# Gradient turns moved from TensorE to DMA transposes, and weight loads cut into pieces, in the training step of a four-layer stack

## The chip, the cores and the metric

The kernel runs on one core of one Trainium2 chip. The metric is the device time of one execution in microseconds (us). The core has a TensorE (PE, with its weight loads shown as PEld), a VectorE (DVE), a ScalarE (ACT), a GpSimd (POOL), a SyncE (SP), and 16 DMA engines.

## The reference

```python
def A(x, wqkv, wo):                       # linear attention, H=32 heads of 16
    q, k, v = split(x @ wqkv)
    phi = lambda t: where(t > 0, t + 1, exp(t)) + 1e-6
    kv, z = phi(k)^T v, sum(phi(k))       # per head
    return concat(phi(q) kv / (phi(q) z + 1e-6)) @ wo
def B(x, w_gate, w_up, w_down):           # gated feed-forward
    return (sigmoid(x @ w_gate) * (x @ w_up)) @ w_down
def fwd(x):
    x = x + A(layernorm(x)); x = x + B(layernorm(x))
    x = x + A(layernorm(x)); x = x + B(layernorm(x))
    return x
out, vjp = jax.vjp(fwd, x, wqkv, wo, w_gate, w_up, w_down)
return out, *vjp(grad_out)
```

This is a sketch of the reference in short form. x is 1 x 2048 x 512 in bfloat16, the feed-forward width is 1376. Both attention layers (numbered 0 and 2) share weights, and so do both feed-forward layers (1 and 3). The outputs are the stack's output and the gradients of x and of the five weight matrices.

## The kernel before

Tokens lie in 16 tiles of P = 128 (NST = 16), four to a batch of BT = 512 (NB = 4, NBLK = 4 batches); 512 features are NDC = 4 blocks of 128; the width 1376 is NFC = 11 chunks of 128. PE, ACT, DVE and POOL work in an order that is written out by hand. All DMAs are issued on SP's one queue; their order there comes from the scheduler by its own estimates, a DMA waits until the one eight before it on SP has landed (eight lanes), and SP issues in order, so that a DMA that waits holds up all behind it. In the trace landings come in order of issue. tile_pool buffers ("bufs") bound how far a producer may run ahead.

The stages in order, with the profile's times in us: forward of layers 0 and 1 until 215, of layers 2 and 3 until 407; backward of layer 3 (BBwd, `first`) 407 to 532; backward of layer 2 (ABwd, "A2") first half 530 to 612, second half to 694; then weight-gradient work, backward of layer 1 (BBwd) 735 to 855; backward of layer 0 (ABwd, "A0") first half 855 to 943, second half to 1000; the remaining weight gradients to the end.

*Forward.* `ab_fwd` does a feed-forward layer in pairs of token tiles; `gu` (L1070) makes g and u for a unit of two chunks (CUNITS, six units to a pair), ACT makes ssd_t and oms from g (L1086, L1087), DVE and POOL hhT and the second half of ssd_t (L1088, L1089), and ssd_t goes to sv_ssd in DRAM (L1092). ssd_t has 3 buffers, tr_stg (L1097, the staging of transposed operands that are stored as sv_hdd and sv_hdl) has 2. In layer 3 `turn_weights` issues, one at a time, the jobs of `wT_dmas_b` (L455), which load transposed weights for the backward pass: among them wuT and wgT, in pieces of chunks 0 to 5 (768 KB) and 6 to 9 (512 KB).

*Feed-forward backward.* `BBwd.run` goes over four batches and 11 chunks u each. `D(n)` makes dhh_ps (L1385) from the turned gradient gT and the weights, two chunks ahead (LOOK = 2), so that the next batch's gT is first read at u = 9; `H` accumulates dh_ps (L1417). gT is made by `make_gT` (L1347): eight PE transposes for each half batch and an ACT copy, at u = 5 and 6 (7 and 8 for the last batch of layer 3). Its source gstage is loaded from grad_out in layer 3 (`load_g`), and in layer 1 cast by ACT from the fp32 residual gradient (`cast_g`, u = 1 to 4), which also stores it to sv_gbf in DRAM (L1345). While H runs, sv_hdd and sv_hdl are stored from tr_stg (L1042), and ssd and h_ld are loaded.

*Attention backward, first half.* `ABwd.first` goes over 16 token tiles (steps): `dp_make` (L1758, dp_ps from gT and MT), `gT_make` for the next tile (four PE transposes L1750, an ACT copy L1751, two buffers), `g_cast` two tiles ahead (ACT, the bfloat16 gradient), and the elementwise work on phq_ld, which is stored as sv_dq (L1823). pqn is loaded by batches (L1837). Each step ends with a *unit* of weight-gradient work from `p2_gen`: 16 matmuls p_ps<-p_set (L1694), four units to a job; p_set holds a job's operand and is loaded two jobs ahead into two buffers (from sv_dkT as four transposing DMAs L1560, from sv_hdd L1571, from sv_hdl as four DMAs L1578); the results go out by dw_stg and dwp (L1648). At the end comes GT_ps (L1870), a sum over all 16 g tiles. The second half loads turned operands by transposing DMAs (pkT_ld L1900, dqT_ld L1904).

Of the kernel before, what the change touches and what calls it, by code (L numbers as in the profile page):

```python
# [9 lines left out]
BF16 = mybir.dt.bfloat16  # L10
# [444 lines left out]
def wT_dmas_b(k):  # L455
    nc = k.nc
    view = lambda d: d.rearrange("(c p) f -> p c f", p=P)
    parts, h = [], F // 2
    for r0, r1, c0 in ((0, h, 0), (h, F, WDT)):
        parts.append((k.wdT[:, WDT:NDC, r0:r1], k.w_in["wd"][r0:r1, WDT * P:D],  # L460
                      [(view(k.wT["wdT"][c0 * P:(c0 + 2) * P, :]), k.wdT[:, c0:c0 + 2, :])]))
    jobs = wT_dmas(k, parts)
    for nm, t in (("wu", k.wuT), ("wg", k.wgT)):
        for c, e in ((0, 6), (6, NFC - 1)):
            jobs.append(lambda nm=nm, t=t, c=c, e=e: nc.sync.dma_start(out=t[:, c:e, :],
                                                                       in_=view(k.wT[nm + "T"][c * P:e * P, :])))
        jobs.append(lambda nm=nm, t=t: nc.sync.dma_start(out=view(k.wT[nm + "T"][(NFC - 1) * P:, :]),
                                                         in_=t[:, NFC - 1:, :]))
    return jobs
# [580 lines left out]
def ab_fwd(k, A, ln, fill, nxt=None, out_cb=None, bwd=None):  # L1050
# [3 lines left out]
    with ExitStack() as ctx:  # L1054
        work = ctx.enter_context(tc.tile_pool(name=f"bf_work{l}", bufs=2, reuse_waits="tile"))
        wide = ctx.enter_context(tc.tile_pool(name=f"bf_wide{l}", bufs=2, reuse_waits="tile"))
        hhT = {}

        def gu(st, nt, c0, nch, between=None):
# [16 lines left out]
            if held:  # L1076
                ssd = bwd.ssd[0][:, c0:c0 + nch, :, off:off + n]
            else:
                ssd_f = work.tile([P, 2 * BT], BF16, name="ssd_t", bufs=3)
                ssd = ssd_f[:, 0:2 * w].rearrange("p (c a t) -> p c a t", c=nch, a=2)  # L1080
# [14 lines left out]
        def trans(B, g):  # L1095
            c0, nch = CG[g]
            block_transposes(k, work, sv, 0, B, g, hhT[B][:, c0:c0 + nch, :], bufs=2)  # L1097

# [56 lines left out]
        for i in range(1, NPAIR):  # L1155
# [7 lines left out]
            nt = 1 if i < NPAIR - 2 else 2  # L1163
            gu(st, 2, *CUNITS[0])
            A.attn_y(st + 2, "t")
            A.pair_front1(i + 2)
# [7 lines left out]
            if l == 3 or i % 2 == 0:  # L1174
                turn_weights()
                if l == 3 and i > 3:
                    turn_weights()
            if i > 1:
                down_mm(st - 2)
            ln.apply(st + 2)  # L1180
            if last:
                trans(NBLK - 1, 0)
            gu(st, 2, *CUNITS[3])
            down_mm(st - 1, "t")
            ln.apply(st + 3)
# [3 lines left out]
            if last:  # L1189
                trans(NBLK - 1, 1)  # L1190
                if bwd is not None:
                    bwd.make_gT(0, 0)
            gu(st, 2, *CUNITS[4])
            ln.stage_T([st + 2, st + 3], bank="t")
            A.pair_front3(i + 2)
            after(st - 2)
            if last and bwd is not None:
                bwd.make_gT(0, 1)
            gu(st, 2, *CUNITS[5])
            fills((nf + 1) // 3, "vector")  # L1200
            if l == 1 and last:
# [108 lines left out]
class BBwd:  # L1310
# [20 lines left out]
    def load_g(self, B):  # L1331
# [3 lines left out]
        t = self.G[B] = self.G.get(B) or self.alloc(False, "stg", [P, NB, D], "gstage", 2)  # L1335
        if self.first:
            nc.sync.dma_start(out=t[:], in_=dram_batch(k.g_in, B))

    def cast_g(self, B, j):
# [91 lines left out]
    def run(self, nxt, hooks={}, rest=None, fill=None):  # L1431
# [3 lines left out]
        with ExitStack() as ctx:  # L1435
# [27 lines left out]
            for B in range(NBLK):  # L1463
                end = B == NBLK - 1
                for u in range(NFC):
                    n = B * NFC + u
                    close = u == NFC - 1
                    behind = self.first and B == 2 and u == 9
                    if close and end:
                        nxt.gT_make(0, "ln")  # L1470
                    if not close and not behind:
                        self.D(n + self.LOOK)
                    self.H(B, u)
                    if behind:
                        self.D(n + self.LOOK)
                    if close and not end:
# [10 lines left out]
                    if not end:  # L1487
# [3 lines left out]
                        if late and u == 3:  # L1491
                            self.load_g(3)
                        if u in ((7, 8) if late else (5, 6)):
                            self.make_gT(B + 1, 0 if u in (5, 7) else 1)
                    if u in (7, 8):
# [227 lines left out]
class ABwd:  # L1723
# [20 lines left out]
    def gT_make(self, st, bank="t"):  # L1744
        k = self.k
        if st < NST:
            self.gTs[st] = self.hold.tile([P, NDC, P], BF16, name="gT", bufs=2)
            ps = ps_tile(k, bank, [P, NDC, P], BF16, "gT_ps")
            for c in range(NDC):
                k.nc.tensor.transpose(ps[:, c, :], self.g[st][:, c * P:(c + 1) * P], k.ident[:])  # L1750
            k.nc.scalar.copy(self.gTs[st][:], ps[:])  # L1751

    def dp_make(self, st):
# [19 lines left out]
    def first(self, fill):  # L1773
# [10 lines left out]
        with tc.tile_pool(name=f"ab_all{l}", bufs=1, reuse_waits="tile") as allp, \  # L1784
# [41 lines left out]

            self.g_cast(2)
            load_ph(0)
            load_ph(1)
            weights = self.weights = k.load_a_weights(l)  # L1830
            for st in range(NST):
# [9 lines left out]
                if st > 0:  # L1841
                    self.dp_make(st)
                    self.gT_make(st + 1)
                    self.g_cast(st + 2)
                    self.cneg_make(st, small.tile([P, H], F32, name="cneg"))
                T["cneg"] = self.cneg
                T["cneg_bf"] = small.tile([P, H], BF16, name="cneg_bf", bufs=DZLAG + 3)
# [189 lines left out]

DZLAG = 4
SMALL = (("G", D), ("kvbd", P), ("dkvbd", P))

# [65 lines left out]
```

## Time and profile before

| | us |
|---|---|
| runs | 1132.63, 1131.10, 1133.29 |
| median of the runs | 1132.63 |
| profiled execution | 1131.85 |
| span of the profiled execution | 1130.1 |
| busy PE, PEld, DVE, ACT, POOL | 1094.4, 673.3, 718.7, 501.9, 468.1 |
| granted clock of TensorE, mean | 0.997 |

The span runs from the first to the last instruction in the trace of one execution; 1.75 us of its time lie outside. A group's row has the line, engine, operation and tiles, then its busy time, the mean ns of one, and the idle time in front of it with what ended it. A row of a timeline has start, duration, engine, line, tiles and how many instructions it holds; in brackets is the idle time before the first, with its releaser. In SP's rows the duration is the time that issuing took; a row of DMA issues ends with the median time from issue to landing. The clock of TensorE is granted by a throttle, as a share of full speed.

### The profile page before, as it was taken

To read this page: it belongs to the slowest core of one execution; us is meant where nothing else is said; L and a number is where in the kernel's file an instruction comes from. 1 tells how busy PE (TensorE), PEld (TensorE's weight loads), DVE (VectorE), ACT (ScalarE), POOL (GpSimd) and SP (SyncE) were. 2 spreads that over 40 slices of the span, in tenths; PEclk is the share of its full clock that TensorE was granted. 3 is DMA by queue.
4 is the path that set the end of the run, shared out by engine and by line. 5 is a ranking of instruction groups with operands and counts; after the bars stand their busy time and mean duration, and the time that the engine had idled before them with its cause. 6 is when DMAs were issued, how large, how long until landed. Compare 5 with 4: busy or idle time off the path is not lost. (4 is left out here: it accounts for less than half of the span.)

```text
span 1130.1 us, 20199 instructions
## 1 busy us (share of the span) xinstructions
PE 1094.4 (97%) x7453; PEld 673.3 (60%) x7556; DVE 718.7 (64%) x1263; ACT 501.9 (44%) x924; POOL 468.1 (41%) x627
## 2 busy tenths in 40 slices
PE   7999999999999899999999999999999999999998
PEld 4467767546776654444665556544446756555577
DVE  7887887888678567776993640057778955642221
ACT  4676656557656533444552441145545523420001
POOL 3738776433766445776110440047772101420000
PEclk9999999999999999999999999999999999999999
DMA  7955657695666768978789967887768999958997
GB/s 218 319 169 160 199 177 222 198 263 177 173 217 187 235 201 265 303 232 278 214 235 265 280 192 253 296 283 225 224 214 223 268 276 253 258 194 272 274 253 166
DMA packets 342612, 263.02 MB, mean 233 GB/s; under 512 B 105648, under 2 KB 321136, under 8 KB 342512
## 3 DMA queue, kind: packets, MB, share of 16 engines
q1 hardware_dynamic: 342512, 261.72, 79.0%
q8 instruction: 59, 0.97, 0.4%
q14 instruction: 41, 0.34, 0.1%
HBM read 122.62 MB, written 119.47 MB: 214 GB/s over the span
## 5 line engine op out<-in xcount | busy, mean ns | idle before, releaser
L1694 PE MATMUL p_ps<-p_set,p_a 128*128 128x384 bf16 (+2 forms) x1792 | 264.6, 304 | 3.3 <-DMA p_set<-sv_hdd 1.5
L1694 PEld LDWEIGHTS <-p_a 128*128 128x128 bf16 x1792 | 168.7, 96 | 87.2 <-issue 3.4
L1393 POOL TENSOR_TENSOR dd<-dhb,ssd 128x512 bf16<-128x512 bf16 x84 | 96.7, 1156 | 106.1 <-ACT dhb L1391 103.9
L1392 DVE TENSOR_TENSOR dd<-dhh_ps,ssd 128x512 bf16<-128x512 f32 x85 | 57.2, 679 | 123.1 <-ACT dhb L1391 121.3
L1417 PE MATMUL dh_ps<-wuT,dd 128*128 128x512 bf16 (+1 forms) x340 | 129.0, 379 | 0.7
L1089 POOL TENSOR_TENSOR ssd_t<-hhT,oms 128x512 bf16<-128x512 bf16 (+1 forms) x92 | 99.7, 1092 | 71.8 <-DVE hhT L1088 50.4
L1417 PE MATMUL dh_ps<-wgT,dd 128*128 128x512 bf16 (+1 forms) x325 | 123.3, 380 | 0.0
L1417 PEld LDWEIGHTS <-dd 128*128 128x128 bf16 x680 | 66.3, 98 | 79.7
L1070 PE MATMUL g_ps<-hT,wg 128*128 128x256 bf16 (+1 forms) x792 | 93.6, 262 | 6.5 <-ACT oms L1087 5.4
L1709 DVE TENSOR_TENSOR dw_stg<-p_ps,dw_stg 128x384 bf16<-128x384 f32 (+2 forms) x76 | 32.0, 438 | 106.4 <-PE p_ps L1694 99.1
L1070 PE MATMUL u_ps<-hT,wu 128*128 128x256 bf16 (+1 forms) x792 | 93.5, 262 | 3.0 <-DVE hhT L1088 3.0
L1391 ACT CAST dhb<-dhh_ps 128x512 bf16<-128x512 f32 x84 | 48.7, 588 | 99.5 <-PE dhh_ps L1385 86.6
L1088 DVE TENSOR_TENSOR hhT<-u_ps,ssd_t 128x512 bf16<-128x512 f32 (+1 forms) x92 | 57.5, 629 | 51.5 <-ACT ssd_t L1086 49.2
L1086 ACT ACTIVATE ssd_t<-g_ps 128x512 bf16<-128x512 f32 (+1 forms) x92 | 51.7, 562 | 86.6 <-PE g_ps L1070 44.4
L1039 DVE STREAM_TRANSPOSE tr_stg<-dd 128x768 f32<-128x768 f32 (+1 forms) x62 | 86.6, 1437 | 1.1
L1070 PEld LDWEIGHTS <-wg 128*128 128x128 bf16 x792 | 70.1, 98 | 27.2 <-issue 8.0
L1385 PE MATMUL dhh_ps<-gT,wdT 128*128 128x512 bf16 x301 | 77.2, 379 | 1.6 <-DVE dd L1392 0.7
L1105 PE MATMUL y_ps<-wd,hhT 128*128 128x512 bf16 (+1 forms) x337 | 77.7, 380 | 0.8
L1070 PEld LDWEIGHTS <-wu 128*128 128x128 bf16 x792 | 70.9, 98 | 12.0 <-issue 4.6
L1711 ACT CAST dw_stg<-p_ps 128x384 bf16<-128x384 f32 (+2 forms) x76 | 28.0, 385 | 88.6 <-PE p_ps L1694 83.8
L1385 PEld LDWEIGHTS <-wdT 128*128 128x128 bf16 x352 | 33.8, 97 | 41.7 <-issue 3.8
L516 POOL TENSOR_TENSOR rstd_all<-rstd_all,neghalf 128x1 f32<-128x1 f32 x64 | 37.9, 592 | 47.7 <-DVE rstd_all L515 43.1
(256 smaller groups left out, 1919.3 us busy)
## 6 DMA issues: line engine op xcount, KB each, us to landing
sv_hdd<-tr_stg SPq DMA_DIRECT2D x72, 384.0 KB, 4.6
p_set<-sv_hdd SPq DMA_DIRECT2D x18, 1536.0 KB, 7.4
sv_ssd<-ssd_t SPq DMA_DIRECT2D x74, 256.0 KB, 2.6
ssd<-sv_ssd SPq DMA_DIRECT2D x23, 768.0 KB, 5.2
h_ld<-sv_h SPq DMA_DIRECT2D x30, 256.0 KB, 4.1
sv_hdl<-tr_stg SPq DMA_DIRECT2D x24, 256.0 KB, 4.8
p_a<-sv_h SPq DMA_DIRECT2D x12, 512.0 KB, 6.5
p_set<-sv_hdl SPq DMA_DIRECT2D x24, 256.0 KB, 4.9
```

The source lines that it names most:

```text
L1039: nc.vector.transpose(t[:, :, 0:n * P].bitcast(F32).rearrange("p q (a j) -> p q a j", a=2 * n), src.rearrange("p c x -> p (c x)").bitcast( ...
L1070: nc.tensor.matmul(ps[:, ci * n:(ci + 1) * n], lhsT=w_sb[:, kc, (c0 + ci) * P:(c0 + ci + 1) * P], rhs=hT[:, kc, (st % 2) * P:(st % 2) * P ...
L1086: nc.scalar.activation(ssd[:, :, 0, :], gv, ACT.Sigmoid)
L1088: nc.vector.tensor_tensor(hh, uv, ssd[:, :, 0, :], ALU.mult)
L1089: nc.gpsimd.tensor_tensor(ssd[:, :, 1, :], hh, oms, ALU.mult)
L1105: nc.tensor.matmul(y_ps[:], lhsT=h[0:r, fc, off:off + P], rhs=k.wd[0:r, fc, :], start=(fc == 0), stop=(fc == NFC - 1))
L1385: nc.tensor.matmul(ps[:], lhsT=k.wdT[:, jc, u * P:(u + 1) * P], rhs=self.gT[B][:, jc, :], start=(jc == 0), stop=(jc == NDC - 1))
L1391: nc.scalar.copy(dhb[:], ps[:])
L1392: nc.vector.tensor_tensor(self.dd[ng][:, 0, c, :], ps[:], self.ssd[ng][:, c, 0, :], ALU.mult)
L1393: nc.gpsimd.tensor_tensor(self.dd[ng][:, 1, c, :], dhb[:], self.ssd[ng][:, c, 1, :], ALU.mult)
L1417: nc.tensor.matmul(self.acc[j][:], lhsT=dd[0:r, a, c, j * P:(j + 1) * P], rhs=w[0:r, u, :], start=(u == 0 and a == 0), stop=(u == NFC - 1 ...
L1694: nc.tensor.matmul(ps[:, 0:w], lhsT=lhs[:, s, ic * P:(ic + 1) * P], rhs=rhs, start=(s == 0), stop=(s == NST - 1))
```

## The change

It has four parts.

1. `wT_dmas_b` loads wuT and wgT in five pieces of two chunks (256 KB) each, so that there are 15 jobs in place of 9, and `ab_fwd` in layer 3 issues them after units 0 (from the second pair), 2, 3 and 5, up to four to a pair, in place of one or two after unit 2.
2. In layer 1's forward, ssd_t comes from a pool of its own with 5 buffers, and tr_stg has 4.
3. Feed-forward backward: gT is no longer turned on PE, except for layer 1's first batch. A new `turn_g` issues two transposing DMAs (256 KB each) for a batch, in layer 3 from grad_out in DRAM, within `load_g` ahead of gstage's load, and in layer 1 from sv_gbf, at u = 6. The exception that put D behind H at one place (`behind`) goes.
4. Attention backward: from tile 3 on, gT is made by a transposing DMA from g in on-chip memory (SBUF) to gT in SBUF, 128 KB each, issued three tiles ahead (GLEAD = 3), with three gT buffers and the cast four tiles ahead; tiles 0 to 2 stay on PE.

The changed program has 216 PE transposes (and as many weight loads) fewer and 46 DMAs more on SP (26 in the attention part, 14 in the feed-forward part, 6 more pieces). In SP's order, the layer-1 turns of batch 0's run are `sv_gbf; ssd; sv_hdd x2; gT x2`, and of the next two `sv_gbf; h_ld; gT; ssd; sv_hdd x2; gT`. In A2 the first attention turn stands right behind the load of pqn; in A0 turns 4 to 12 stand among the loads of p_set, phq_ld and p_a. A turn of tile st + 3 waits for `dp_make(st)`, which frees its buffer, and for its cast.

```diff
@@ -461,7 +461,8 @@
                       [(view(k.wT["wdT"][c0 * P:(c0 + 2) * P, :]), k.wdT[:, c0:c0 + 2, :])]))
     jobs = wT_dmas(k, parts)
     for nm, t in (("wu", k.wuT), ("wg", k.wgT)):
-        for c, e in ((0, 6), (6, NFC - 1)):
+        for c in range(0, NFC - 1, 2):
+            e = c + 2
             jobs.append(lambda nm=nm, t=t, c=c, e=e: nc.sync.dma_start(out=t[:, c:e, :],
                                                                        in_=view(k.wT[nm + "T"][c * P:e * P, :])))
         jobs.append(lambda nm=nm, t=t: nc.sync.dma_start(out=view(k.wT[nm + "T"][(NFC - 1) * P:, :]),
@@ -1054,6 +1055,7 @@
     with ExitStack() as ctx:
         work = ctx.enter_context(tc.tile_pool(name=f"bf_work{l}", bufs=2, reuse_waits="tile"))
         wide = ctx.enter_context(tc.tile_pool(name=f"bf_wide{l}", bufs=2, reuse_waits="tile"))
+        more = ctx.enter_context(tc.tile_pool(name=f"bf_more{l}", bufs=5, reuse_waits="tile")) if l == 1 else None
         hhT = {}
 
         def gu(st, nt, c0, nch, between=None):
@@ -1076,7 +1078,7 @@
             if held:
                 ssd = bwd.ssd[0][:, c0:c0 + nch, :, off:off + n]
             else:
-                ssd_f = work.tile([P, 2 * BT], BF16, name="ssd_t", bufs=3)
+                ssd_f = (more or work).tile([P, 2 * BT], BF16, name="ssd_t", bufs=5 if more else 3)
                 ssd = ssd_f[:, 0:2 * w].rearrange("p (c a t) -> p c a t", c=nch, a=2)
             oms_f = work.tile([P, BT], BF16, name="oms")
             oms = oms_f[:, 0:w].rearrange("p (c t) -> p c t", c=nch)
@@ -1094,7 +1096,7 @@
 
         def trans(B, g):
             c0, nch = CG[g]
-            block_transposes(k, work, sv, 0, B, g, hhT[B][:, c0:c0 + nch, :], bufs=2)
+            block_transposes(k, work, sv, 0, B, g, hhT[B][:, c0:c0 + nch, :], bufs=4 if l == 1 else 2)
 
         def down_mm(st, bank="y"):
             y_ps = ps_tile(k, bank, [P, D], F32, "y_ps")
@@ -1162,6 +1164,8 @@
                     trans(*pend.pop(0))
             nt = 1 if i < NPAIR - 2 else 2
             gu(st, 2, *CUNITS[0])
+            if l == 3 and i > 1:
+                turn_weights()
             A.attn_y(st + 2, "t")
             A.pair_front1(i + 2)
             after(st - 3)
@@ -1173,14 +1177,14 @@
             gu(st, 2, *CUNITS[2])
             if l == 3 or i % 2 == 0:
                 turn_weights()
-                if l == 3 and i > 3:
-                    turn_weights()
             if i > 1:
                 down_mm(st - 2)
             ln.apply(st + 2)
             if last:
                 trans(NBLK - 1, 0)
             gu(st, 2, *CUNITS[3])
+            if l == 3:
+                turn_weights()
             down_mm(st - 1, "t")
             ln.apply(st + 3)
             A.pair_prod(i + 3)
@@ -1188,15 +1192,13 @@
             trs(nt)
             if last:
                 trans(NBLK - 1, 1)
-                if bwd is not None:
-                    bwd.make_gT(0, 0)
             gu(st, 2, *CUNITS[4])
             ln.stage_T([st + 2, st + 3], bank="t")
             A.pair_front3(i + 2)
             after(st - 2)
-            if last and bwd is not None:
-                bwd.make_gT(0, 1)
             gu(st, 2, *CUNITS[5])
+            if l == 3:
+                turn_weights()
             fills((nf + 1) // 3, "vector")
             if l == 1 and last:
                 nc.scalar.activation(k.tab[:], k.neg[:], ACT.Exp)
@@ -1334,7 +1336,16 @@
         k, nc = self.k, self.k.nc
         t = self.G[B] = self.G.get(B) or self.alloc(False, "stg", [P, NB, D], "gstage", 2)
         if self.first:
+            self.turn_g(B)
             nc.sync.dma_start(out=t[:], in_=dram_batch(k.g_in, B))
+
+    def turn_g(self, B):
+
+        if B not in self.gT:
+            self.gT[B] = self.alloc(False, "work", [P, NDC, BT], "gT", 2)
+        for half in range(2):
+            self.k.nc.sync.dma_start_transpose(out=self.gT[B][:, :, half * 2 * P:(half + 1) * 2 * P],
+                                               in_=self.sv["gbf"][batch_rows(2 * B + half, 2), :])
 
     def cast_g(self, B, j):
         k, nc = self.k, self.k.nc
@@ -1465,14 +1476,11 @@
                 for u in range(NFC):
                     n = B * NFC + u
                     close = u == NFC - 1
-                    behind = self.first and B == 2 and u == 9
                     if close and end:
                         nxt.gT_make(0, "ln")
-                    if not close and not behind:
+                    if not close:
                         self.D(n + self.LOOK)
                     self.H(B, u)
-                    if behind:
-                        self.D(n + self.LOOK)
                     if close and not end:
                         done = self.ln_begin(B)
                         for i in range(2):
@@ -1490,8 +1498,8 @@
                         late = self.first and B == 2
                         if late and u == 3:
                             self.load_g(3)
-                        if u in ((7, 8) if late else (5, 6)):
-                            self.make_gT(B + 1, 0 if u in (5, 7) else 1)
+                        if u == 6 and not self.first:
+                            self.turn_g(B + 1)
                     if u in (7, 8):
                         self.load_h(B, u - 7)
                     if u == 8 and not (self.first and B == 1):
@@ -1744,11 +1752,16 @@
     def gT_make(self, st, bank="t"):
         k = self.k
         if st < NST:
-            self.gTs[st] = self.hold.tile([P, NDC, P], BF16, name="gT", bufs=2)
+            self.gTs[st] = self.hold.tile([P, NDC, P], BF16, name="gT", bufs=GLEAD)
             ps = ps_tile(k, bank, [P, NDC, P], BF16, "gT_ps")
             for c in range(NDC):
                 k.nc.tensor.transpose(ps[:, c, :], self.g[st][:, c * P:(c + 1) * P], k.ident[:])
             k.nc.scalar.copy(self.gTs[st][:], ps[:])
+
+    def turn_g(self, st):
+        if GLEAD - 1 < st < NST:
+            self.gTs[st] = self.hold.tile([P, NDC, P], BF16, name="gT", bufs=GLEAD)
+            self.k.nc.sync.dma_start_transpose(out=self.gTs[st][:], in_=self.g[st][:])
 
     def dp_make(self, st):
         k = self.k
@@ -1824,7 +1837,8 @@
                                                 in_=T["ph_pair"][:, :, g * GW:(g + 1) * GW])
                     return ins.ins
 
-            self.g_cast(2)
+            for st in range(2, GLEAD + 2):
+                self.g_cast(st)
             load_ph(0)
             load_ph(1)
             weights = self.weights = k.load_a_weights(l)
@@ -1840,9 +1854,11 @@
                 T = dict(st=st, ph=phs[st // NB2][:, st % NB2, :], ph_pair=phs[st // NB2])
                 if st > 0:
                     self.dp_make(st)
-                    self.gT_make(st + 1)
-                    self.g_cast(st + 2)
+                    if st + 1 < GLEAD:
+                        self.gT_make(st + 1)
+                    self.g_cast(st + GLEAD + 1)
                     self.cneg_make(st, small.tile([P, H], F32, name="cneg"))
+                self.turn_g(st + GLEAD)
                 T["cneg"] = self.cneg
                 T["cneg_bf"] = small.tile([P, H], BF16, name="cneg_bf", bufs=DZLAG + 3)
                 nc.gpsimd.tensor_scalar(T["cneg_bf"][:], T["cneg"][:], 1.0, 0.0, ALU.mult, ALU.add)
@@ -2036,6 +2052,7 @@
 
 
 DZLAG = 4
+GLEAD = 3
 SMALL = (("G", D), ("kvbd", P), ("dkvbd", P))
```

## The prediction

> **What bounds the kernel now.** I read the page's first part and DMA row, then the groups of the operations that go, then PE's timeline, SP's timeline and the DMA issues at the places where the new transfers come in.
>
> ```profile
> PE 1094.4 (97%) x7453; PEld 673.3 (60%) x7556; DVE 718.7 (64%) x1263; ACT 501.9 (44%) x924; POOL 468.1 (41%) x627
> DMA  7955657695666768978789967887768999958997
> ```
>
> PE is busy 97% of a span of 1130.1 us: what is taken from PE shortens the kernel, if what replaces it is in time. The DMA row is in tenths per fortieth (28.3 us): the attention parts of the backward pass (slices 19 to 25 and 30 to 34) stand at 7 to 9 already.
>
> The sum goes against the profiled execution, 1131.85 us (span and 1.75 around it); the median of the runs is 0.8 above it.
>
> **What goes: turns on PE.**
>
> ```profile
> L1750 PE MATMUL gT_ps<-ident,g 128*128 128x128 bf16 x128 | 12.4, 219 | 0.0
> 558.80 0.39 PE L1750 MATMUL gT_ps<-ident,g 128*128 128x128 bf16 x4
> 559.02 0.24 PE L1807 MATMUL dz_ps<-cneg_bf,pqn 128*128 128x8 bf16 x4
> 755.15 0.61 PE L1356 MATMUL gT_ps<-ident,gstage 128*128 128x128 bf16 x8
> 755.60 1.03 PE L1385 MATMUL dhh_ps<-gT,wdT 128*128 128x512 bf16 x4
> ```
>
> Four turns hold PE from 558.80 to the next start, 559.02: 0.22 us, with no idle time before them. 26 of the 32 fours go: 26 x 0.22 = **5.7**. Eight turns of a feed-forward half batch hold it 755.15 to 755.60, 0.45. Fourteen of sixteen halves go: 14 x 0.45 = **6.3**. The ACT copies that go with them (40) count nothing: ACT is busy 44%.
>
> **What goes: a stall in the last forward layer.**
>
> ```profile
> 377.39 0.60 ACT L1086 ACTIVATE ssd_t<-g_ps 128x512 bf16<-128x512 f32 x1 [6.00 <-DMA sv_ssd<-ssd_t]
> 378.53 1.87 PE L1070 MATMUL g_ps<-hT,wg 128*128 128x256 bf16 x8 [3.70 <-ACT oms L1087]
> 380.19 1.76 PE L1070 MATMUL u_ps<-hT,wu 128*128 128x256 bf16 x8
> 381.79 0.38 PE L1105 MATMUL y_ps<-wd,hhT 128*128 128x512 bf16 x1
> 378.25:381.66 3.41, 3.13 (x15) 2.23 (x15) 3.31 (x7) 2.83 (x7) 2.28 (x5) 0.50 0.44 146
> ```
>
> ACT can't reuse an ssd_t buffer until its store has landed. That store was issued at 369.59 behind the 768 and 640 KB of weight loads issued at 368.35 and 368.86, and landed at 377.29: 7.7 us, where such stores take 2.6 in the median. PE stands 3.70 us, and the 16 matmuls behind it run at a granted clock of 0.50 (the 0.50 in the window's row), 378.53 to 381.79 = 3.26 us where sixteen otherwise take 1.74: 1.5 more. The change cuts these loads into 256 KB and spreads them from pair 1 on, four to a pair. With 3.70 go 1.04 of the same kind at 340.11, and 0.44 at 407.60, where PE waited for the ACT copy of the first gradient turn, which no longer is there. Sum 3.70 + 1.04 + 1.5 + 0.44 = **6.7**. Below nothing is possible only if the pieces delay another store; pair 1 on has DMA shares below 0.7, so I take 0 as the lower end. The wider pool in layer 1 meets gaps of 3.2 us in all in front of L1070; most end with DVE's hhT and not with a store: I take **1.0** (0 to 3.2).
>
> Gains: 5.7 + 6.3 + 6.7 + 1.0 = **19.7**.
>
> **What it adds, 1: layer-1 feed-forward gradients late.** The turn reads sv_gbf back from DRAM, so it waits for the cast (unchanged), the store's landing, and then its own. On SP it stands behind two sv_hdd stores.
>
> ```profile
> 753.50 0.60 SPq L1345 DMA_DIRECT2D sv_gbf<-gstage  x1
> 763.82 1.03 PE L1385 MATMUL dhh_ps<-gT,wdT 128*128 128x512 bf16 x4
> sv_gbf<-gstage SPq DMA_DIRECT2D x4, 512.0 KB, 5.0
> pkT_ld<-sv_pk SPq DMA_TRANSPOSE x14, 4.3
> ```
>
> The next batch's first dhh_ps needs it at 763.82, less 0.9 for the PE time saved by then: 762.9. Batch 0: the pair follows the hdd stores (which end at 761.62, 0.45 earlier now); its second half is issued at about 762.4 and lands 4.3 later, at 766.7: 3.8 late. Batch 1: store at 783.19, landing 788.2, half 1 behind the next hdd pair (to 790.9), landing 795.2 against 792.6: 2.6. Batch 2: half 1 at 820.7, 825.0 against 822.2: 2.8. Sum 9.2. A PE gap of 3.70 was followed by half clock, one of 1.49 (at 694.08) was not; I price one such window for the 3.8: 1.5. **10.7.** Low end: landings as short as the shortest transposes (3.2): 5.9. High: as the longer ones of 5.6: 9.2 + 3.9 + 1.5 = 14.6. [...] Taking the gbf load ahead of H in the order (the removed `behind`) and the moved load_g cost nothing: DVE is busy 64%.
>
> In layer 3 the turns come from grad_out, 25 us and more before their use, and only the first must wait for a landing (out_t's). I count nothing; the cover is that lead, and if it were gone each would cost what the rows above cost, 3 to 4.
>
> **Adds, 2: 13 turns in A2's first half, within SBUF.** No row shows a transpose from SBUF to SBUF. The nearest are those from DRAM: on SP 1.25 us each (128 KB and 256 KB alike), to landing 4.0 to 4.3. A step there is 2.8 us (3.8 for wide units), the lead three steps, and SP is busy 22 of 46 us, so most turns arrive. The first does not: it is issued right behind pqn (542.60, 6.0 in the median, landed 548.15), landings come in order of issue, so it lands at about 548.7; dp_ps of step 3 started at 546.56, now 546.3. **2.4** (0 to 11; the upper end with 2.7 of SP for each: 22 + 35 = 57 us in 46).
>
> **Adds, 3: 13 turns in A0's first half.**
>
> ```profile
> 880.42 3.23 SPq L1560 DMA_TRANSPOSE p_set<-sv_dkT  x2
> 888.74 0.60 PE L1694 MATMUL p_ps<-p_set,p_a 128*128 128x256 bf16 x4 [0.82 <-DMA p_set<-sv_dkT]
> 889.86 0.60 PE L1694 MATMUL p_ps<-p_set,p_a 128*128 128x256 bf16 x4 [0.52 <-DMA p_set<-sv_dkT]
> 891.48 3.59 SPq L1578 DMA_DIRECT2D p_set<-sv_hdl  x4
> 860.00:943.00 83.00, 80.55 (x669) 56.74 (x678) 63.00 (x136) 34.14 (x69) 9.07 (x17) 1.00 0.96 258
> ```
>
> Here SP issues without a break, 866.0 to 876.6 and 879.4 to 900.6, idle only 2.8 between, its issues waiting for the transfers eight ahead of them; the DMA share is 0.96 (the last but one column), and PE already stands for p_set. Nine turns (4 to 12) stand ahead of the hdl set or among what it waits for: 9 x 1.25 = 11.3, less 2.8 of idle time = 8.5. The set landed at 899.96 in the trace with 0.3 to spare, and PE comes 9 x 0.22 = 2.0 earlier: it waits 8.5 - 0.3 + 2.0 = **10.2**. Low end, turns issued in 0.37 as plain loads are: 3.3 - 2.8 - 0.3 + 2.0 = 2.2. High end, as the longest transposing issue here (868.80, 2.69): 24.2 - 2.8 - 0.3 + 2.0 = 23.1. I take 1.25: the commonest transposing issue (dqT_ld, pkT_ld), and half of these rows have the turn's size. The wait of the turn for dp_make(st) and for the cast stops everything behind it on SP (phq loads, dq stores, p_set), and through p_set, PE; that is inside the 2.2 to 23.1.
>
> The casts, now four steps ahead, are on ACT at 44% and count nothing. None of the three costs can be below nothing: what PE saves is booked above, and no transfer is taken away here.
>
> Costs: 10.7 + 2.4 + 10.2 = 23.3. Net 23.3 - 19.7 = 3.6 later: 1135.4, and with the 0.8 **1136 us**. Its own range, costs halfway to their ends: 1129 to 1145.
>
> **The rivals.** *Faster: the turns are in time.* If they land as the shortest rows do (3.2) and cost SP as little as a plain load: 5.9 in layer 1, nothing in A2, 2.2 in A0: gains 19.7 less 8.1 = 11.6, so 1132.6 - 11.6 = **1121**. For it: all turns but three per layer have over 7 us of lead. Against: SP's unbroken row in A0. It decides at 762.9 (half 1 landed or not) and where a turn's lead of three steps, 7.6 us, covers issue and landing.
>
> *Much slower: a turn within SBUF holds SP longer than one from DRAM.* With 2.7 each: A0 23.1, A2 11, layer 1 10.7 = 44.8 - 19.7 = 25 later, **1158**; from 1.9 on SP's work in A2 (22 + 13 x 1.9 = 46.7) fills its 46 us and every further 0.1 costs 1.3 per stage. For it: no row shows this direction. Against: halving the size left the issue at 1.25. [...] Every transposing row of this trace without a wait is at 1.2 to 1.3, so this has 0.04.
>
> *The pieces do not free the ssd stores* (the wait is for bandwidth, not order): 6.2 of the gain is missing, **1142**. The pieces move the same bytes, but earlier, at a lower share.
>
> **How the numbers follow.** Forecast with the third rival 0.48, faster rival 0.24, much slower 0.28 (of it 0.1 beyond 1164, the 0.04 among them). A measurement of this kernel can tell about 0.2% (2.3 us) from no change. Faster 0.24; within 0.2%, the lower part of the forecast's range (1130.4 to 1134.9), 0.10; slower 0.66. The range leaves out a tenth on each side: 1121 to 1164.
>
> **What would show it.** PE idle of 2 to 4 us at L1385 at the start of the batches in layer 1, released by a DMA into gT; at L1758 near 546; at L1694 near 899 by p_set. No 3.70 gap near 378. SP durations of 1.25 in the row of the new turns. It is wrong if that row shows 0.4 or 2.7 and more, or if L1694 waits nowhere longer than before.

## The result and the profile after

| | before | after |
|---|---|---|
| median of the runs, us | 1132.47 | 1159.61 |
| all runs, us | 1131.10 to 1133.29 | 1157.25 to 1164.06 |
| span of the profiled execution, us | 1130.1 | 1158.2 |
| granted clock, mean | 0.997 | 0.985 |

The changed kernel is slower: its ratio to before is 1.0246, 95% interval 1.0213 to 1.0278. That lies in the stated range (1121 to 1164) and on the forecast's side, but far from the forecast of 1136: the loss is 27 us, not 4. By stages of the two traces (each from the first dhh_ps, dp_ps, GT_ps or dpk_ps of a stage to that of the next):

| stage | before | after | difference |
|---|---|---|---|
| forward, to the first dhh_ps | 407.6 | 395.4 | -12.2 |
| BBwd 3 | 125.4 | 127.9 | +2.5 |
| A2, first half to GT_ps | 54.7 | 60.5 | +5.8 |
| BBwd 1 | 120.3 | 142.7 | +22.5 |
| A0, first half to GT_ps | 58.3 | 69.2 | +10.9 |
| all else | 363.9 | 362.5 | -1.5 |

The page's first row, of the kernel after:

```profile
PE 1093.1 (94%) x7240; PEld 664.2 (57%) x7340; DVE 720.3 (62%) x1263; ACT 475.9 (41%) x884; POOL 468.6 (40%) x627
```

PE executes 213 recorded matmul rows fewer than before and is busy nearly as long (1094.4 before): what the turns gave back was spent again in matmuls at half clock. Over the windows of half clock, PE's busy time sums to 29.5 us after and 6.3 before; half of the difference, 11.6, is time lost, where the prediction put the turns' PE time at 5.7 + 6.3 = 12.0. The groups after that touch the change (busy us, mean ns, then idle us in front and its releasers):

```profile
L1396 PE MATMUL dhh_ps<-gT,wdT 128*128 128x512 bf16 x300 | 79.9, 390 | 18.0 <-DMA gT<-sv_gbf 16.2 <-DVE dd L1403 1.0
L1771 PE MATMUL dp_ps<-MT,gT 128*128 128x512 bf16 x113 | 32.3, 395 | 19.5 <-DMA gT<-g 18.6 <-issue 0.2
L1702 PE MATMUL p_ps<-p_set,p_a 128*128 128x384 bf16 (+2 forms) x1792 | 266.9, 306 | 0.9 <-DMA p_set<-sv_hdd 0.9
```

PE stands 16.2 us for layer 1's turns and 18.6 us for the attention turns. It stands *less* for p_set than before, where the same group (L1694 there) had this row:

```profile
L1694 PE MATMUL p_ps<-p_set,p_a 128*128 128x384 bf16 (+2 forms) x1792 | 264.6, 304 | 3.3 <-DMA p_set<-sv_hdd 1.5 <-DMA p_set<-sv_dkT 1.3 <-DVE dw_stg L1709 0.5
```

That is 2.8 us for p_set before and 0.9 after: the wait that was forecast there is not there. Layer 1's three gaps, in PE's timeline after:

```profile
762.88 1.44 PE L1396 MATMUL dhh_ps<-gT,wdT 128*128 128x512 bf16 x3 [4.05 <-DMA gT<-sv_gbf]
800.85 1.46 PE L1396 MATMUL dhh_ps<-gT,wdT 128*128 128x512 bf16 x3 [6.18 <-DMA gT<-sv_gbf]
838.37 1.03 PE L1396 MATMUL dhh_ps<-gT,wdT 128*128 128x512 bf16 x2 [5.92 <-DMA gT<-sv_gbf]
```

SP's timeline ahead of the second of them (start, time to issue):

```profile
790.19 1.25 SPq L1347 DMA_TRANSPOSE gT<-sv_gbf  x1
791.54 0.52 SPq L1377 DMA_DIRECT2D ssd<-sv_ssd  x1
792.16 1.21 SPq L1043 DMA_DIRECT2D sv_hdd<-tr_stg  x2
793.42 4.25 SPq L1347 DMA_TRANSPOSE gT<-sv_gbf  x1
```

The first half turn landed at 793.28, in time. The second stands behind 768 KB of ssd and two stores of 384 KB; it landed at 800.81, right behind them (797.51, 798.62, 799.73). The same picture in A2, SP's and PE's timelines after:

```profile
565.69 0.37 SPq L1579 DMA_DIRECT2D p_set<-sv_hdd  x1
566.17 1.21 SPq L1764 DMA_TRANSPOSE gT<-g  x1
...
573.58 0.61 PE L1771 MATMUL dp_ps<-MT,gT 128*128 128x512 bf16 x2 [1.89 <-DMA gT<-g]
```

The p_set load of 1536 KB landed at 572.96, the turn behind it at 573.53. The turn was issued 5.5 us before PE was ready for it (571.69) and took 7.4 us to land: the lead went on someone else's bytes.

Last, the windows of both kernels over the first halves of A2 and A0, two rows before and then, after, one of half clock and the same two stages (the last three columns are granted clock, DMA share, GB/s):

```profile
532.97:587.66 54.69, 54.20 (x435) 36.52 (x442) 50.25 (x99) 32.70 (x75) 9.07 (x18) 1.00 0.68 204
857.49:915.74 58.25, 56.48 (x507) 43.57 (x513) 54.61 (x113) 31.67 (x66) 9.26 (x18) 1.00 0.97 265
```

```profile
799.48:806.31 6.83, 5.24 (x12) 1.94 (x14) 1.01 (x2) 0.59 (x1) 1.15 (x1) 0.50 0.79 252
523.29:583.82 60.53, 53.30 (x382) 34.01 (x388) 53.19 (x105) 26.18 (x61) 9.36 (x19) 0.97 0.88 223
875.68:944.85 69.17, 56.95 (x452) 41.34 (x459) 55.74 (x115) 25.10 (x53) 9.26 (x18) 0.95 1.02 250
```

The DMA share is the mean over the 16 engines of the time that the packets started in the window took, so it can pass 1. A0 had no DMA time to give (0.97); A2 had a third (0.68) and lost 5.8 us all the same. Each gap of layer 1 runs into 6.83 us at half clock, which begin 1.0 to 1.4 us before the gap ends.

### The profile page after: what moved, and what is told of

It is laid out like the page before. It is cut to its first block, busy times and chain, and to the rows that moved or that the text cites. A ratio compares the mean times of both kernels' runs of the same rounds, so it can differ in the third digit from the quotient of the medians.

```text
span 1158.2 us, 19792 instructions
## 1 busy us (share of the span) xinstructions
PE 1093.1 (94%) x7240; PEld 664.2 (57%) x7340; DVE 720.3 (62%) x1263; ACT 475.9 (41%) x884; POOL 468.6 (40%) x627
## 5 line engine op out<-in xcount | busy, mean ns | idle before, releaser
L1428 PE MATMUL dh_ps<-wuT,dd 128*128 128x512 bf16 (+1 forms) x339 | 132.5, 391 | 4.1 <-DVE junk L1251 3.3
L1428 PE MATMUL dh_ps<-wgT,dd 128*128 128x512 bf16 (+1 forms) x329 | 128.4, 390 | 0.1
L1428 PEld LDWEIGHTS <-dd 128*128 128x128 bf16 x680 | 68.2, 100 | 89.3 <-issue 14.1
L1396 PE MATMUL dhh_ps<-gT,wdT 128*128 128x512 bf16 x300 | 79.9, 390 | 18.0 <-DMA gT<-sv_gbf 16.2
L1719 ACT CAST dw_stg<-p_ps 128x384 bf16<-128x384 f32 (+2 forms) x76 | 28.1, 386 | 93.0 <-PE p_ps L1702 89.2
L1864 POOL TENSOR_SCALAR cneg_bf<-cneg 128x32 bf16<-128x32 f32 x32 | 16.8, 525 | 104.5 <-DVE cneg L1783 96.0
```

The costliest lines, as they stand in the source:

```text
L1396: nc.tensor.matmul(ps[:], lhsT=k.wdT[:, jc, u * P:(u + 1) * P], rhs=self.gT[B][:, jc, :], start=(jc == 0), stop=(jc == NDC - 1))
L1428: nc.tensor.matmul(self.acc[j][:], lhsT=dd[0:r, a, c, j * P:(j + 1) * P], rhs=w[0:r, u, :], start=(u == 0 and a == 0), stop=(u == NFC - 1 ...
```

## The experiments

Times differ somewhat between chips (the kernel before took 1134.93, 1134.74 and 1136.22 us in the median on the three used here), so each kernel is compared with the kernel before on its own chip.

| kernel | median, us | before, us | ratio, 95% interval |
|---|---|---|---|
| e1_fwd, forward part alone | 1123.69 | 1134.93 | 0.9900 [0.9884, 0.9916] |
| e2_bb1pe, layer 1's turns on PE | 1141.85 | 1134.93 | 1.0070 [1.0050, 1.0090] |
| e3_attpe, attention turns on PE | 1149.54 | 1134.93 | 1.0124 [1.0104, 1.0144] |
| e4_lead5, attention turns five tiles ahead | 1162.45 | 1134.93 | 1.0243 [1.0219, 1.0267] |
| e5_bothpe, e2 and e3 together | 1121.85 | 1134.74 | 0.9890 [0.9866, 0.9914] |
| e6_sbturn, e5 and layer 1 turned within SBUF | 1131.38 | 1134.74 | 0.9969 [0.9943, 0.9995] |
| e7_l3late, e5 and layer 3's last turn later | 1123.23 | 1134.74 | 0.9897 [0.9867, 0.9927] |
| e1p_pieces, weight loads in pieces alone | 1126.38 | 1134.74 | 0.9930 [0.9906, 0.9954] |
| e9_hook, e5 and MT, p_a loaded later | 1119.17 | 1136.22 | 0.9849 [0.9824, 0.9873] |
| e1_again, the forward part alone, again | 1124.22 | 1136.22 | 0.9893 [0.9871, 0.9914] |

**e1_fwd and e1p_pieces: the forward part.** e1_fwd is the kernel before with parts 1 and 2 of the change, e1p_pieces with part 1 alone:

```diff
-        for c, e in ((0, 6), (6, NFC - 1)):
+        for c in range(0, NFC - 1, 2):
+            e = c + 2
...  # e1_fwd also:
-                ssd_f = work.tile([P, 2 * BT], BF16, name="ssd_t", bufs=3)
+                ssd_f = (more or work).tile([P, 2 * BT], BF16, name="ssd_t", bufs=5 if more else 3)
```

> The kernel before with the two forward parts alone (weight loads in pieces, spread over pairs 1 to 4; the wider ssd_t and tr_stg in layer 1); all gradient turns stay on PE. In the trace after, the span up to the first dhh_ps is 12.2 us shorter (407.60 to 395.42), of which 0.9 are two halves of turns that left it. If these parts are independent of the rest, 11.3 less than before: about 1121. If part of the 12.2 needs the turn to be off PE and off ACT, as the prediction's sum had it (6.7 less the 0.44, and 1.0), about 1125. No gap of 3.70 near 378 in either case.

> The kernel before with the weight loads in pieces alone, without the wider pools of layer 1. In the traces the layer-1 forward went from 134.97 to 131.83 (3.1) and layer 3's from 139.94 to 132.81 (7.1). If the pools made the first and the pieces the second, this is 7 to 8 less than before; the prediction gave layer 1's part 1.0, so that this would be 10 of the 11.2.

1.0% less than before, 11.2 us by the medians: the larger expectation. With the pieces alone, layer 3's forward (first to last g_ps) went from 139.94 to 132.47 and layer 1's stayed (134.97 and 135.14); with the pools as well, layer 1's went to 131.83. So the pieces bring some 7 us and the pools 3.1 (single profiled executions), which the prediction had at 6.7 and 1.0. No window of half clock is left in layer 3's forward.

**e2_bb1pe: layer 1's turns back on PE.**

```diff
-                        if u == 6 and not self.first:
-                            self.turn_g(B + 1)
+                        if u in (5, 6) and not self.first:
+                            self.make_gT(B + 1, u - 5)
```

> The changed kernel with layer 1's turns (batches 1 to 3) back on PE at u = 5 and 6. Theory: the three gaps at L1396 (4.05, 6.18, 5.92) and the three half-clock windows of 6.83 us behind them are all that BBwd 1 lost; the stage goes back from 142.7 to 120.3 us: 1159.6 - 22.5 = about 1137. Rival: the waits move, because SP's other loads there were late as well (stores, ssd); then the stage keeps over 125 us and the time is over 1142.

BBwd 1 took 120.29 us, to the hundredth what it took before. So the turns by DMA made all of its 22.5, and no wait moved elsewhere within the stage when they left. The gaps (16.2) and what half clock cost behind them (8.4, worked out below), less 2.7 of PE time for turns, come to 21.9 of it. The total is 5 us above the 1137: this chip's kernel before is 2.5 slower, and in the profiled execution A2's half was 62.6 in place of 60.5.

**e3_attpe: attention turns back on PE.**

```diff
-                    if st + 1 < GLEAD:
-                        self.gT_make(st + 1)
-                    self.g_cast(st + GLEAD + 1)
+                    self.gT_make(st + 1)
+                    self.g_cast(st + 2)
...
-                self.turn_g(st + GLEAD)
```

> The changed kernel with all attention turns back on PE (two buffers, cast two tiles ahead). Theory: the first half of A2 goes from 60.5 back to 54.7 and that of A0 from 69.2 to 58.3, so 1159.6 - 5.8 - 10.9 = about 1143. Rival: A0's first half was made longer by its later start against the queue (what came before it was moved by 18 us) and not by the turns: A0's half stays over 62 us and the time is over 1146.

A2's half went to 56.2, A0's to 58.6, though A0 still started some 15 us later than before: the turns made the loss, not the later start. The total fell by less than expected: in its profiled execution the stretch from A0's first dpk_ps on took 3.3 us more than in the kernel after, and the forward pass 2.0 more, without a cause that these runs isolate.

**e4_lead5: the same turns, issued two tiles earlier.** Here the theory was that a turn only has to be issued early enough.

```diff
-            self.gTs[st] = self.hold.tile([P, NDC, P], BF16, name="gT", bufs=GLEAD)
+            self.gTs[st] = self.far.tile([P, NDC, P], BF16, name="gT", bufs=LEAD)   # LEAD = 5
...
-                self.turn_g(st + GLEAD)
+                for t in (range(GLEAD, LEAD + 1) if st == 0 else (st + LEAD,)):
+                    self.turn_g(t)
```

> The changed kernel with the attention turns issued five tiles ahead in place of three, into five buffers of their own (so that a turn waits for the dp_make five tiles before it); tiles 0 to 2 stay on PE. Theory (a turn lands in order behind the large loads issued just before it, and its lead of three tiles is 1.5 to 3.5 us too short there): two more steps are 5 to 7 us, the seven gaps of 1.1 to 3.5 us at dp_ps and the half-clock windows near 560, 888 and 918 go, 6.7 + 10.4 of idle time and about 5 of half clock: about 1138. Rival (the prediction's: SP or the queue is full, and what a turn takes is taken from p_set): the wait turns up at p_set or stays at gT, over 1150.

The theory fell: no gain (ratio 1.0243; after, on its chip, 1.0246). The groups of e4_lead5 say where the wait went:

```profile
L1702 PE MATMUL p_ps<-p_set,p_a 128*128 128x384 bf16 (+2 forms) x1792 | 269.4, 306 | 13.9 <-DMA p_set<-sv_hdd 6.4 <-DMA p_set<-sv_dkT 4.6 <-DMA p_set<-sv_hdl 1.2
L1771 PE MATMUL dp_ps<-MT,gT 128*128 128x512 bf16 x128 | 34.1, 390 | 1.2 <-ACT gT L1759 0.6 <-DMA gT<-g 0.5
```

The turns are in time (0.5 us where it was 18.6), and p_set is late instead: 12.2 us where it was 0.9. One queue serves both; here the lead only decided which of the two PE waits for. A0's half took 66.3 (after: 69.2) at a DMA share of 1.03, with 7.0 us of waits for p_set; A2's took 60.7 (60.5), with one gap of 3.76 for p_set and two half-clock windows.

**e10_copy and e11_half: what a turn costs in a full queue.** Both start from e2_bb1pe, with one profiled execution each (1132.09 and 1138.47 us, where e2_bb1pe's median is 1141.85 on another chip). e10_copy moves the same bytes without turning them; e11_half turns only the odd tiles by DMA.

```diff
-            self.k.nc.sync.dma_start_transpose(out=self.gTs[st][:], in_=self.g[st][:])
+            self.k.nc.sync.dma_start(out=self.gTs[st][:].rearrange("p c t -> p (c t)"), in_=self.g[st][:])
...  # e11_half instead:
-        if GLEAD - 1 < st < NST:
+        if GLEAD - 1 < st < NST and st % 2:
```

> As e2_bb1pe (the changed kernel with layer 1's turns on PE), but the attention DMAs copy g to gT within SBUF without turning it, so that the attention gradients from tile 3 on are of unturned tiles. Bytes, order and waits stay. Theory (what costs is turning: small packets that hold all the DMA engines for 1.1 to 1.2 us per 128 KB): A2's first half goes from 62.6 to under 55 and A0's from 68.4 to under 60, near what they are with the turns on PE, and the DMA share in A2's half falls from 0.83 to about 0.7. Rival (the copy in itself, its place in the queue and its waits cost): both halves stay over 58 and 64.

> As e2_bb1pe, but only the odd tiles from 3 on (7 of 13 in each attention layer) are turned by DMA, the even ones on PE. Theory (A0's first half is bound by the DMA engines, each turn 1.1 us of all of them): A0's half takes 58.2 + 7/13 of the 10 more = about 64. Rival (single late turns behind large loads): the loss hangs on which tiles meet a large load (tiles 3, 9, 11 and 15 of the changed kernel's waits are odd), and stays above 66 or falls below 61.

| first half, us | turns on PE (e5) | 13 turns (e2) | 13 copies (e10) | 7 turns (e11) |
|---|---|---|---|---|
| A2 | 54.5 | 62.6 | 58.7 | 61.8 |
| A0 | 57.5 | 68.5 | 65.2 | 65.1 |

The windows of A0's half, in the order of the columns:

```profile
848.50:905.99 57.49, 56.55 (x508) 43.67 (x514) 54.43 (x113) 31.74 (x66) 9.24 (x18) 1.00 0.96 270
857.49:925.94 68.45, 57.28 (x464) 41.33 (x462) 55.98 (x115) 25.32 (x53) 9.26 (x18) 0.95 1.01 257
849.84:915.08 65.24, 56.08 (x463) 40.91 (x461) 55.86 (x115) 25.29 (x53) 9.24 (x18) 0.97 1.01 270
855.21:920.26 65.05, 56.95 (x487) 42.36 (x485) 54.94 (x113) 28.28 (x59) 9.25 (x18) 0.97 0.98 252
```

Each is one execution, and with the turns on PE the halves took 54.5 to 56.2 and 57.5 to 58.7 in the traces of this study, so that a microsecond between two cells says nothing. e10_copy goes with the rival (58.7 and 65.2, over its 58 and 64): in A0 the mere copies cost 7.8 of the 11.0, so that most of the price is a transfer more in a full queue, and turning adds 3.2. In A2 the copies cost about half of the 8.1. The turns' packets (512 of 256 B each) took 0.70 us of the sixteen engines per turn in the kernel after's A2, not the 1.1 to 1.2 that the theory takes, which is the rise of the two stages' DMA time (length times share) from before to after, 14 and 16 us, over 13 turns.

e11_half leaves both sides standing. In A0 seven turns cost 7.6, somewhat over the proportional 5.9, and the stage's 65.1 lies midway between the theory's 64 and the rival's 66. Its waits look like those of A2: 7.3 of the 7.8 us for gT are two gaps (3.91 and 3.38) at single tiles that landed right behind pqn and p_set. In A2 seven turns cost 7.3, nearly as much as thirteen: two gaps (2.28 and 3.07), again right behind pqn and p_set, with a half-clock window behind each. What sets the stages apart is the room: A0's DMA time (length times share, 55, 69, 66 and 64 us along the table) is about as long as the stage itself, while A2's share stays between 0.70 and 0.84. That a lack of DMA time and not the order behind lumps makes A0's loss is thus supported and not shown; no run moved the turns ahead of those loads, and none used a second queue.

**e5_bothpe and e7_l3late: layer 3.** e5_bothpe joins the edits of e2 and e3. e7_l3late also pins load_g(3), which holds the last turns:

```diff
-                            self.load_g(3)
+                            with tc.issue_after(self.last_ssd):
+                                self.load_g(3)
```

> The changed kernel with the attention turns and layer 1's turns back on PE: what is left is the forward part and layer 3's turns by DMA. The forward part alone took 11.2 off. Theory: layer 3's turns save 0.9 in the forward pass and cost BBwd 3 2.5 to 3.8 (a gap of 3.3 to 4.1 and a half-clock window, because SP stands 6.3 us at the two turns of the last batch and the stores of tr_stg behind them come late): 8 to 10 less than before. Rival, the prediction's (layer 3's turns are hidden): 11.2 + 3.6 = 15 less than before.

> As e5_bothpe, with the turns of layer 3's last batch (and its gstage load) pinned behind the second ssd load of batch 2, past the loads of p_a and the first stores. Theory: SP no longer stands at them ahead of those stores, the gap at L1428 near 465 and its half-clock window go, BBwd 3 takes 125.4 - 2.7 = 122.7: about 6 less than e5_bothpe, 14 to 15 less than before. Rival: moved later, the turns themselves are late at u = 9: a gap at dhh_ps released by gT, BBwd 3 over 125.

e5_bothpe stands where e1_fwd does (0.989 and 0.990): layer 3's turns by DMA gained nothing. BBwd 3 took 128.7 where e1_fwd took 125.4. The cause given in the expectations (stores of tr_stg held up on SP by the last batch's turns) was wrong: with the turns moved past those stores, e7_l3late's gap at L1428 was still 3.87 us and BBwd 3 took 129.3. Its DVE timeline names the cause, and the windows 428 to 468 us of e1_fwd and then of e7_l3late show the ground:

```profile
464.96 0.75 DVE L1251 SCALAR_TENSOR_TENSOR junk<-dh_ps,rstd_all,h_ld 128x512 bf16<-128x512 f32 x1 [4.48 <-DMA h_ld<-sv_h]
```

```profile
428.00:468.00 40.00, 39.80 (x197) 18.34 (x196) 29.90 (x42) 18.61 (x37) 27.57 (x32) 1.00 0.82 269
```

```profile
428.00:468.00 40.00, 35.86 (x159) 16.02 (x161) 26.46 (x40) 15.61 (x33) 25.65 (x30) 0.96 0.94 306
```

DVE's layer-norm sums wait 4.48 us for h_ld, and the next batch's dh_ps waits for those sums to empty PSUM. The kernel after has the same waits, DVE's of 3.92 us before 463.54 and PE's of 3.31 before 464.35. h_ld stands behind the loads of MT and p_a in a queue whose share went from 0.82 to 0.94.

**e9_hook: make room there.**

```diff
-        B3.run(A2, {(1, 8): open_a1, (3, 5): open_sets})
+        B3.run(A2, {(2, 2): open_a1, (2, 5): more_a1, (2, 8): more_a1, (3, 2): more_a1, (3, 5): open_sets})
...  # open_a1 loads MT and the first batch of p_a, more_a1 one batch more, each behind the last ssd load:
+            with tc.issue_after(k.last_ssd):
+                b_load_batch(k, R, w["h3"], k.sv[3]["h"], w["n"])
```

> As e5_bothpe (forward part, and layer 3's turns by DMA, all others on PE), with the loads of MT and p_a (2.5 MB, issued together ahead of the second h_ld of batch 1) spread over batches 2 and 3 behind ssd loads. In e7_l3late the gap at L1428 stayed at 3.9, and DVE stood 4.48 us for h_ld, which landed at 464.84 behind MT and p_a. Theory: the queue is full there (DMA share 0.94), h_ld lands in order behind those loads; with them later the gap and the half-clock windows go and BBwd 3 takes 125.4 - 2.7 = 122.7, about 6 less than in e5_bothpe (128.7). Rival: any 2.5 MB more in this stretch delays something that is needed (ssd, tr_stg's stores), and BBwd 3 stays over 125.

> The same kernel as e1_fwd (forward part alone), to stand beside e9_hook on the same chip: about 11 less than before. By the theory for e9_hook, that one is 3.6 below this one (0.9 in the forward pass, 2.7 in BBwd 3); by its rival it is not below it.

As the theory has it. The window of e9_hook's whole BBwd 3:

```profile
395.56:518.15 122.59, 122.31 (x577) 55.73 (x575) 87.99 (x110) 46.19 (x92) 83.95 (x86) 1.00 0.93 293
```

122.6 us, full clock, at a share of 0.93 over the whole stage: the turns fit when nothing urgent stands behind a lump (a large transfer or several issued together). e9_hook is 5.05 us below e1_again on the same chip (all runs 1115.65 to 1119.79 against 1122.55 to 1126.65), where the theory had 3.6, and with 1119.17 the fastest kernel of this study, 1.5% below before. That the spread loads alone made BBwd 3 shorter was not run, but its trace leaves them little: in e1_again PE stood idle for 0.20 us of that stage (125.37 us, full clock).

**e6_sbturn: layer 1 without the trip through DRAM.**

```diff
                             self.cast_g(B + 1, u - 1)
+                            if not self.first:
+                                self.turn_tile(B + 1, u - 1)   # gT[:, :, tile] <- gstage[:, tile, :], SBUF to SBUF
```

> As e5_bothpe, but layer 1's turns of batches 1 to 3 by DMA from gstage in SBUF, one of 128 KB per token tile right behind its cast (u = 1 to 4), in place of PE: no trip through sv_gbf. Theory (in the changed kernel the turns were late because the store, its landing and the ssd and sv_hdd transfers ahead in the queue all come before them): the turns now have 5 chunks, 12 us and more, no gap at dhh_ps, BBwd 1 takes 120.3 - 2.7 = 117.6, 2.7 less than e5_bothpe. Rival (a turn costs the DMA engines 1.2 us each wherever it is issued, and delays ssd or the stores of tr_stg behind it): BBwd 1 over 121, at or above e5_bothpe, the wait at ssd or tr_stg.

The rival holds. The turns were in time (no wait for gT in the stage) and BBwd 1 took 125.6, 5.3 more than on PE: what comes late now is tr_stg's stores, as DVE's timeline of e6_sbturn shows:

```profile
765.19 1.09 DVE L1040 STREAM_TRANSPOSE tr_stg<-dd 128x512 f32<-128x512 f32 x1 [4.06 <-DMA sv_hdd<-tr_stg]
```

By the medians e6_sbturn is 9.5 us above e5_bothpe. Its ten runs spread from 1124.26 to 1136.82, and the profiled one (1135.41) also took 5.1 longer in the forward pass, which the edit does not touch; no run here isolates that part.

## Why the prediction was right or wrong

**Right in sign and range, by a sum that was mis-sized.** The forecast's own range, 1129 to 1145, missed. Costs halfway to their upper ends (12.65 + 6.7 + 16.65 = 36.0) would have put its upper end at 1149, and that misses too. That 1159.6 lies inside 1121 to 1164 is luck: the upper end came from the chance of "much slower", whose mechanism did not occur. From the forecast to the trace 24.5 us are missing (28.1 for 3.6): 14.5 in layer 1, 6.3 in A2, 3.6 in A0 and 5.2 in layer 3, less 3.6 more gained in the forward pass and 1.5 in all else.

*Turns that leave PE.* Stages whose waits were removed confirm the size: BBwd 3 came down by 2.8 in e9_hook against e1_again (six halves of 0.45 are 2.7).

*Forward.* Forecast 7.7, measured 11.2 in e1_fwd. The pieces were right (one stretch, 330 to 360 us, stood at a DMA share of 0.75 before, not below 0.7, without harm); layer 1's pools were taken at 1.0 because their gaps named DVE's hhT, and gave 3.1. The named releaser stood itself behind the buffers: in that layer before, DVE waited 18.9 us for ACT's ssd_t, and ACT 13.3 for ssd_t buffers whose stores had not landed; in e1_fwd ACT waited for none.

*Layer 1, the term that failed most.* Forecast 10.7, measured 22.5 + 2.7 = 25.2. The first gap was 4.05 for a forecast 3.8, by the right path. The second and third were 6.2 and 5.9 for 2.6 and 2.8: the step that failed is the second half's landing as its issue plus a median of 4.3. It stood on SP 4.25 and 3.58 (a risk that the trace before showed: 19 of its 92 transposing issues took over 2 us, the longest 6.14) and landed behind the ssd load and the stores issued just before it. And the half clock was priced at one window of 1.5; it was 6.83 us three times, behind all three gaps, of which 5.9, 5.5 and 5.5 lay behind the gap, half of that lost: 8.4.

*A2.* Forecast 2.4, measured 5.8 + 2.9 = 8.7. The first late turn behind pqn came as described (1.63). "So most turns arrive" failed: the same rule of landing in order was not applied to p_set, behind which two more turns came 3.08 and 1.89 late.

*A0.* Forecast 10.2, measured 10.9 + 2.9 = 13.8. The resource was right, the full queue, and the place was wrong: PE waited for gT (11.7 us in this stage) and not for p_set. By its own last line (wrong "if L1694 waits nowhere longer than before") this step of the prediction failed: that line's wait for p_set fell from 2.8 to 0.9. e4_lead5 moved the wait to the forecast's place with a longer lead.

*Layer 3, counted at nothing.* It cost 2.5 + 2.7 = 5.2. The cover that I named, a lead of 25 us, covers the turns themselves; what I left out is who stands behind them in a queue at a share of 0.84: h_ld, by 3.9 us.

*The rivals.* "Faster" fell at each place where it was to be decided: half 1 missed u = 9, and three steps did not cover the queue. "Much slower" gave 1158, close to the result, by a mechanism that the runs refute: a turn within SBUF holds SP 1.22 us (median of 26; four took over 2), close to the 1.25 of the DRAM rows, not 2.7. The 0.04 stood for a turn that holds SP so long that the time passes 1164; no run shows one: the longest of the 26 held it 4.31 us. "The pieces do not free the ssd stores" is refuted by e1p_pieces: layer 3's forward lost 7.5 us and its half-clock window.

Landings came in order of issue in the traces of both kernels: of the 785 recorded DMAs of the kernel after and the 739 of the kernel before, none landed ahead of the one issued before it. I had read the order from the trace and used it at one place out of four.

## What to carry to other kernels

Before moving work from a busy engine to DMAs, price each new transfer by the queue at its place: in both traces what was issued in the few microseconds ahead of it landed first, and what was issued behind it landed later, so the lateness is in bytes ahead and not in the transfer's own median (7.4 us for a turn behind 1536 KB of p_set, 4.3 in the median). A longer lead did not help where the queue itself was full; it handed the wait to the next load (p_set in e4_lead5). And a turn that is itself in time can make another transfer late (h_ld in e5_bothpe, tr_stg's stores in e6_sbturn). Where turns by DMA did pay, in one stage out of four, it was after other loads had been spread out of their way.

## What the runs showed of the hardware

- A DMA transpose of 128 KB from SBUF to SBUF held SP for 1.22 us in the median of the kernel after (1.19 at the least), one of 256 KB from DRAM for 1.25 at the least. The turn within SBUF landed 2.4 us after the start of its issue at the least, 4.3 in the median, 7.4 behind the 1.5 MB of a p_set.
- A transposing issue can stand for microseconds by itself (4.25, 3.58, 4.31 us) where the queue holds large transfers, while the plain loads and stores around it took 0.4 to 1.0. It is not the wait for the DMA eight before it: that one had landed 5.7, 5.8 and 1.9 us before these issues began. They ended within 0.2 us of the landing of a transfer ahead of them (797.67 and 797.51, 835.13 and 835.12, 884.02 and 884.09); why, no run here shows.
- In the traces of before and after the half-clock windows last 3.41 or 6.83 us (but for the last, which the span's end cuts), and the length of a gap does not settle them: a gap of 2.57 us (at 888.13) was followed by one, one of 3.09 us (at 910.22) was not. What settles them is where a gap lies on a fixed grid of 3.41 us, on which all half-clock windows of a trace start. These are the grid's windows around the two gaps, in the kernel after:

```profile
884.81:888.22 3.41, 0.84 (x8) 0.51 (x7) 3.24 (x7) 0.51 (x2) 0.81 (x2) 1.00 1.28 178
905.29:908.70 3.41, 1.84 (x17) 1.40 (x15) 2.89 (x6) 0.75 (x2) 0.52 (x1) 1.00 1.25 197
908.70:912.11 3.41, 1.89 (x18) 1.53 (x20) 0.38 (x1) 1.00 (x2) 0.00 (x0) 1.00 0.73 172
```

PE idles 2.57 us in the first and 1.57 and 1.52 in the other two, over which the longer gap is split. In the traces of before and after, all 11 of the grid's windows at full clock in which PE idled 2.04 us or more were followed by one at half clock, and none of the 646 in which it idled 1.89 or less (windows wholly within the span). A window at half clock was followed by another when PE idled 0.95 us or more in it (3 times), and by full clock at 0.40 or less (9 times). In these traces a late transfer thus turned dear once PE waited about 2 us within one such window.
